# Sliding-window attention, then a squared-ReLU layer: two groups of x turned in another PSUM bank, and a new planned order

## The chip, the cores and the metric

The kernel runs on one core of a Trainium2 chip. The metric is device time in microseconds (us); of the kernel before, three timed runs gave a median of 291.02 us (290.34 to 291.29). About 0.9 us, 0.3%, is the least difference that a measurement of this kernel tells from none.

## What is computed

The reference, cut to what matters. There are 8 batches of 8 heads, 576 positions and 64 elements a head; the output of attention, laid out as 4608 tokens by 512, is the x of the second part.

```python
scores = (q @ k.T) / sqrt(64)                      # q, k, v: 8 x 8 x 576 x 64
scores = where(abs(i - j) <= 32, scores, -1e9)     # a band of 65 keys
attn   = softmax(scores) @ v
x      = attn.transpose(0, 2, 1, 3).reshape(4608, 512)
h      = x @ w_in                                  # 512 x 2048
g      = maximum(h, 0) ** 2
out    = g @ w_out                                 # 2048 x 512, float32 out
```

## The kernel before

**Attention** goes by groups G = 0 to 23 of 192 positions, three to a batch, all eight heads at once. The steps of a group have these names in the text below, and these lines in the profile:

- Loads of k, q and v issued by GpSimd (POOL; `load_qk` L477, `load_pair` L509, `load_v` L526). They cast float32 to bfloat16 on the way.
- Turning k and q: groups 0 to 5 on TensorE (turn k10 is that of k, batch 1, group 0, so G = 3; L568) into a PSUM bank, which ScalarE (ACT, L596 and L601) or VectorE (DVE, L599) then empties. From group 6 on the DMA queue of SyncE (SP) transposes them (L608).
- S, the scores: on PE, L649 for groups 0 to 2, in two halves SA and SB, and L697 after that. X is the exponential on ACT (L674, L711), M the multiplication with the mask on DVE (L679, L719, L725).
- PA and PB, the product with v on PE (L753). R and N on DVE (L772, L775) divide it by its sums and write xa and xb. Between PA and PB, Z clears half of a bank (ACT L783 or DVE L785). So PB can start only after N of PA and Z.
- T, the turning of x: group 0 in the banks ht0 and outp1; groups 1 and 2 on PE (Ta L833, Tb L838), into one bank, which ACT empties into the tile xt (XT, L850); from group 3 on by SP's transposes (L854, L857).

**The first product** (A, L879) takes x in tiles of 192, later 256 tokens, in eight blocks of eight matmuls a tile; each block fills a bank that ACT empties with a ReLU (L885). The square follows on DVE (L893) or ACT (L895). In the first three tiles three banks take turns (ht0, ht1, outp1). The first block of a tile needs the turned x of its last group: A384.0, the first of the third tile, needs XT of group 2.

**The second product** works on pairs of 128 tokens with seven products instead of eight (P1 to P7, L965; sums of g on DVE, L951), but for the first pair, which takes plain products (B, L905) into outp0 and outp1.

PSUM has eight banks here: four are attention's tile at (scores in all four, PA and PB in banks 2 and 3), two are ht0 and ht1, two are outp0 and outp1.

**The order** is not written out. Every step is recorded with a key (its due time in units of 64 tokens), a cost, and what it reads and writes; a planner then runs the five engines and the DMA queues in a small model, takes on each engine the ready step with the lowest key, and writes the instructions in that order, with waits on semaphores. Offsets per kind of step (OFFS), a penalty on the other engine for steps that may run on ACT or DVE (FLEX), noise on the keys (NOISE, SEEDS) and the modelled DMA rates and delays (QMOVE, TGAP, the SLACKs) all bend that order. An engine works through its instructions strictly in the written order, so a wait holds up all that stands behind it. While PE has little to do in the first 20 us, dummy matmuls (L405) fill it.

Of the kernel before, what the change touches and what calls it, by code (L numbers as in the profile page):

```python
# [19 lines left out]
RING = 1536  # L20
NV, NRAW = 6, 6
TG = 6
# [4 lines left out]
GFAR = 12  # L27
GATE = 'P{}B'
GD = 3
GK = 8.0  # L30
TDKEY = 6
XKEY = (0.2, 0.5)
QMOVE = 14.8
HMOVE = 27
# [12 lines left out]
LANDQ = 2000  # L47
PQ = 100
# [13 lines left out]
SWB = 180  # L62
HWQ = {'k': 'SP', 'q': 'SP'}
HWC = {"k": ("DVE", "ACT"), "q": ("ACT", "DVE")}
TILES = ((192, 2304), (256, 4608))
SEEDS = (54889, 73113, 37345, 76131, 20885, 97248, 47624, 10448, 1997, 7471, 50773, 3305, 47783, 64133, 39018, 28670, 69087, 23028, 92194, 70005)
NOISE = 0.0
NBIAS = 1
PKEY = 2
MKEY = (-9.5, -6.5)  # L70
# [3 lines left out]
IOTA = -1  # L74
OPENING = [('k', 1), ('w1', 0), ('v', 0, 0), ('q', 1), ('v', 0, 1), ('q', 2), ('w1', 1), ('q', 5),
# [7 lines left out]
PSTEP = 0.4  # L83
SLEAD = 2.5
MOE = -1
SQBEG = 768
# [6 lines left out]
TWKEY = 6  # L93
# [263 lines left out]
class Gen:  # L357
# [103 lines left out]

    def gate(self, G):
        if G < 6:
            return None
        return self.p.named[GATE.format(G - GD)] if G >= GFAR else self.moe
# [12 lines left out]

    def load_hw(self, t, g, key):

# [19 lines left out]
    def load_pair(self, t, b, g, key):  # L502

        t0, n = KC[g] if t == "k" else (192 * g, 192)
        h = n // 2
        G = 3 * b + g
        pr, raw = self.PR[t][G % NPR], self.RAW[t][G % NRAW]
        s = (self.q if t == "q" else self.k)[b][:, t0:t0 + n, :].rearrange("h (p r) d -> p h (r d)", r=2)
        self.p.rec("POOL", lambda e: e.dma_start(pr[0:h, :].rearrange("p (h c) -> p h c", c=128), s), writes=[("pr", t, G % NPR)],  # L509
                   dma=(f"{t}p{G % NPR}", G), key=key, dur=500 + 3 * h, move=(h // 2, PMOVE), name=f"{t}{b}{g}",  # L510
                   slack=LSLACK1 if b else 0)
        self.p.rec("DVE", lambda e: e.tensor_copy(raw[0:h, :, :].rearrange("p r (h d) -> p r h d", d=64),
                                                  pr[0:h, :].rearrange("p (h r d) -> p r h d", r=2, d=64)),
                   reads=[("pr", t, G % NPR)], writes=[("raw", t, G % NRAW, x) for x in range(2)], key=3 * G - LEAD - PKEY if b == 0 else key, dur=430,
                   name=f"c{t}{b}{g}")

    def load_v(self, b, g, key, js=(0, 1)):
        G = 3 * b + g
        vt = self.V[G % NV]
        for j in js:  # L520
            k0 = 192 * g - 32 + 128 * j
            lo, hi = max(k0, 0), min(k0 + 128, S_)
            if g and j == 0 and G < NVR:
                lo = k0 + 64
            n = hi - lo
            self.p.rec("POOL", lambda e, j=j, lo=lo, hi=hi, k0=k0: e.dma_start(  # L526
                vt[lo - k0:hi - k0, j, :, 0:64], self.v[b, :, lo:hi, :].rearrange("h p d -> p h d")),
                writes=[("v", G % NV, j)], dma=(f"v{G % NV}{j}", G), key=key, dur=500 + 3 * n, move=(n // 2, VMOVE),
                name=f"v{b}{g}{j}", after=self.gate(3 * b + g), slack=LSLACK if b > 1 else LSLACK1 * b)

    def copy_v(self, G, key):
# [86 lines left out]
    def scores(self, G, ws):  # L618
        b, g = divmod(G, 3)
        i = b % 2  # L620
        kt, qt = self.KT[i], self.QT[i]
        key = 3 * G - LEAD + 0.3 * ws[0]
        a = 192 * g
        reg = {w: w if len(ws) == 2 or G < NBIAS else 0 for w in ws}
        if G < NBIAS:
# [57 lines left out]
    def scores_steps(self, G):  # L683
        b, g = divmod(G, 3)
        i = b % 2
        kt, qt = self.KT[i], self.QT[i]
        key = 3 * G - LEAD
        a = 192 * g
        n = G % 2

# [38 lines left out]
    def pv(self, G, w):  # L729
        b, g = divmod(G, 3)  # L730
        n = 2 * G + w
        key = 3 * G - LEAD + 0.3 * w + 0.1
# [55 lines left out]

    def xturn(self, G):
        xa, xb = self.XA[G % 3], self.XB[G % 3]  # L790
        key = 3 * G - LEAD + 0.5
# [70 lines left out]
    def mm1(self, t0, n, ds, key):  # L862
# [26 lines left out]
        if SQBEG <= t0 < SQEND and k % SQMOD[1] in SQMOD[0]:  # L889
# [4 lines left out]
                   reads=[("rt", k % 4)], writes=wr, key=key, dur=dve(c), name=f"g{t0}.{d0}",  # L894
                   alt=("ACT", lambda e: e.activation(gt[:, d0:d0 + len(ds), r:r + n], rr, ACTF.Square), act(c), "g")  # L895
                   if "g" in FLEX else None)

    def mm2(self, u, seg, key):
        op, gt = self.OUTP[u % 2], self.GT
# [158 lines left out]
    def build(self):  # L1058
# [40 lines left out]
        for G in range(NG):  # L1099
            b, g = divmod(G, 3)  # L1100
            if b > 1:
                key = 3 * G - LEAD - (GK if G >= GFAR else AHEAD)
                for t in "kq":
                    at(key, self.load_pair if G < TG else self.load_qk, t, b, g, key)
                at(key, self.load_v, b, g, key)
                if g and G < NVR:
                    key = 3 * G - LEAD - 0.5 if G >= VCS else key
                    at(key + 0.01, self.copy_v, G, key - VKEY if G >= VCS else key)
            for t in "kq":
                key = 3 * G - LEAD - (0.6 if G < TG else TDKEY)  # L1110
                at(key, self.turn_pe if G < TG else self.turn_dma, t, b, g, key)
            for ws in ((0,), (1,)) if G < NSPLIT else ():
                at(3 * G - LEAD + 0.3 * ws[0], self.scores, G, ws)
            if G >= NSPLIT:
                at(3 * G - LEAD, self.scores_steps, G)
            for w in range(2):
                at(3 * G - LEAD + 0.3 * w + 0.1, self.pv, G, w)
            at(3 * G - LEAD + 0.5, self.xturn, G)
        t0 = 0
        while t0 < NTOK:  # L1120
            n = next(n for n, end in TILES if t0 < end)
            m = min(512 // n, 4)
            for d in range(0, 16, m):
# [57 lines left out]
```

## Time and profile before

| | |
|---|---|
| median of three timed runs | 291.02 us |
| the profiled execution | 292.3 us |
| its span, first to last instruction | 290.1 us |
| mean granted TensorE clock | 0.999 |
| busy share: PE, DVE, ACT, POOL | 98%, 72%, 71%, 37% |
| read from HBM, written | 36.70 MB, 9.44 MB |
| DMA rate over the span | 159 GB/s |

The profile is of one execution, which took 292.3 us; 2.2 us of them lie outside the span. PE's busy time is that of matmuls whose ends are modelled, and consecutive matmuls overlap, so a wait of PE shows in full only in the distance between starts. Times of single instructions are given from the span's start.

### The profile page before, as it was taken

What the parts mean: (1) busy time and instruction counts of PE and PEld (TensorE: products, weight loads), DVE (VectorE), ACT (ScalarE), POOL (GpSimd) and SP (SyncE); (2) the same over time, 40 slices, a digit from 0 to 9 for tenths busy, and PEclk for the clock granted to TensorE, in tenths of its full rate; (3) what the DMA queues carried; (4) which work ended last, traced back from release to release, by engine and by line L of the source; (5) the groups of instructions that cost most, each with busy time, mean ns of one, the idle gap of its engine ahead of it and who ended that gap; (6) DMA issues with size and microseconds to landing.
All of it is one profiled execution on the core that took longest, in us unless ns stands there. A gap on an engine that the chain in (4) does not pass through costs nothing.

```text
span 290.1 us, 8378 instructions
## 1 busy us (share of the span) xinstructions
PE 283.0 (98%) x3426; PEld 245.6 (85%) x3430; DVE 208.2 (72%) x451; ACT 206.3 (71%) x379; POOL 107.0 (37%) x143
## 2 busy tenths in 40 slices
PE   7988999999999999999999999999999999999996
PEld 2467885889999999999998898888888888988885
DVE  6668779878687878686968886766876877735263
ACT  3379987586989988778776677758687638688520
POOL 8986660141566066326415435606236000000000
PEclk9999999999999999999999999999999999999999
DMA  9999999999999999999999999999999921202024
GB/s 161 188 194 186 197 178 139 200 135 173 113 143 209 129 165 119 173 171 143 124 150 189 150 127 169 131 190 90 169 106 139 143 91 29 84 18 76 0 75 145
DMA packets 160645, 39.97 MB, mean 138 GB/s; under 512 B 149984, under 2 KB 156256, under 8 KB 160608
## 3 DMA queue, kind: packets, MB, share of 16 engines
q0 software_dynamic: 106016, 17.93, 94.2%
q1 hardware_dynamic: 49552, 12.47, 31.4%
q10 hardware_dynamic: 5040, 9.05, 9.8%
q8 instruction: 27, 0.44, 0.7%
q14 instruction: 10, 0.08, 0.1%
HBM read 36.70 MB, written 9.44 MB: 159 GB/s over the span
## 4 chain that ended last, share of the span: by engine, by line
PE 87%; DVE 6%; ACT 3%; DMA 1%; issue 1%; ACTq 0%; DVEq 0%
PE ht L879 39%; PE outp L965 29%; PE at L965 4%; PE at L753 4%; PE at L697 3%; PE outp L405 2%; DMA oe<-in_q_dram 1%; PE at L879 1%; PE outp L905 1%; PE outp L879 1%; DVE xa L775 1%; DVE tw L932 1%; ACT qt L596 1%; DVE kt L599 1%; ACT e L674 1%
## 5 line engine op out<-in xcount | busy, mean ns | idle before, releaser
L879 PE MATMUL ht<-xt,w 128*128 128x192 bf16 (+1 forms) x1248 | 135.9, 258 | 0.0
L879 PEld LDWEIGHTS ht<-xt,w 128*128 128x128 bf16 x1248 | 109.3, 98 | 7.9 <-ACT qt L596 0.3
L885 ACT ACTIVATE rt<-ht 128x384 bf16<-128x384 f32 (+1 forms) x156 | 82.4, 534 | 36.4 <-PE ht L879 31.4
L477 POOL DMA_DIRECT2D kraw<-in_k_dram x36 | 27.7, 775 | 113.1 <-PE at L753 54.6
L895 ACT ACTIVATE gt<-rt 128x384 bf16<-128x384 bf16 (+1 forms) x116 | 65.3, 569 | 4.4 <-ACT rt L885 1.5
L526 POOL DMA_DIRECT2D v<-in_v_dram x48 | 37.7, 793 | 0.0
L965 PE MATMUL outp<-w,gt 128*128 128x256 bf16 x240 | 31.1, 273 | 0.0
L965 PE MATMUL outp<-tw,gt 128*128 128x256 bf16 x240 | 31.1, 273 | 0.0
L965 PE MATMUL outp<-tw,ss 128*128 128x256 bf16 x240 | 30.5, 273 | 0.3 <-DVE ss L951 0.2
L893 DVE TENSOR_TENSOR gt<-rt 128x384 bf16<-128x384 bf16 (+1 forms) x52 | 19.9, 386 | 13.5 <-ACT rt L885 13.0
L477 POOL DMA_DIRECT2D qraw<-in_q_dram x36 | 27.7, 773 | 0.0
L711 ACT ACTIVATE e<-at 128x1024 bf16<-128x1024 f32 x21 | 21.4, 1020 | 7.3 <-PE at L697 7.0
L965 PEld LDWEIGHTS outp<-tw,ss 128*128 128x128 bf16 x240 | 22.9, 98 | 3.1 <-issue 0.3
L965 PEld LDWEIGHTS outp<-w,gt 128*128 128x128 bf16 x240 | 23.0, 98 | 3.0 <-ACT oe L915 0.5
L965 PEld LDWEIGHTS outp<-tw,gt 128*128 128x128 bf16 x240 | 22.9, 98 | 2.5
L985 DVE TENSOR_TENSOR oe<-outp,uu 128x256 f32<-128x256 f32 (+1 forms) x30 | 16.6, 554 | 8.2 <-ACT rt L885 4.9
L719 DVE TENSOR_TENSOR pt<-e,mask 128x1024 bf16<-128x1024 bf16 x21 | 14.5, 691 | 11.1 <-ACT e L711 11.0
L753 PE MATMUL at<-v,pt 128*128 128x66 bf16 x384 | 20.1, 194 | 0.1
L753 PEld LDWEIGHTS at<-v,pt 128*128 128x128 bf16 x384 | 17.8, 98 | 2.2 <-ACT at L783 0.4
L725 DVE TENSOR_TENSOR pt<-em,mask 64x512 bf16<-64x512 bf16 x42 | 17.6, 420 | 1.7 <-ACT em L714 0.3
L775 DVE TENSOR_TENSOR xa<-at,rs 64x512 bf16<-64x512 f32 x24 | 16.7, 695 | 1.1
L775 DVE TENSOR_TENSOR xb<-at,rs 128x512 bf16<-128x512 f32 x24 | 16.5, 686 | 0.8
(112 smaller groups left out, 321.8 us busy)
## 6 DMA issues: line engine op xcount, KB each, us to landing
out_dram<-oe ACTq DMA_DIRECT2D x34, 256.0 KB, 4.0
qraw<-in_q_dram POOLq DMA_DIRECT2D x36, 96.0 KB, 6.2
w<-in_moe_w_in_dram POOLq DMA_DIRECT2D x4, 512.0 KB, 11.1
v<-in_v_dram POOLq DMA_DIRECT2D x16, 128.0 KB, 7.8
w<-in_moe_w_out_dram POOLq DMA_DIRECT2D x4, 512.0 KB, 17.7
v<-in_v_dram POOLq DMA_DIRECT2D x16, 96.0 KB, 7.0
kraw<-in_k_dram POOLq DMA_DIRECT2D x12, 112.0 KB, 5.5
kraw<-in_k_dram POOLq DMA_DIRECT2D x12, 96.0 KB, 4.4
```

The lines of the kernel that those rows point to most:

```text
L477: self.p.rec("POOL", lambda e, j=j: e.dma_start(raw[0:h, j, :].rearrange("p (h d) -> p h d", h=8), s[:, j]), writes=[("raw", t, G % NRAW, ...
L526: self.p.rec("POOL", lambda e, j=j, lo=lo, hi=hi, k0=k0: e.dma_start(vt[lo - k0:hi - k0, j, :, 0:64], self.v[b, :, lo:hi, :].rearrange("h ...
L711: self.p.rec("ACT", lambda e: e.activation(e2[:], self.AT[:, 0:1024], ACTF.Exp, scale=0.125), reads=lo, writes=[("e", n)], key=key, dur=ac ...
L725: self.p.rec("DVE", lambda e, w=w, r=r, x=x, mm=mm: e.tensor_tensor(pt[x:x + 64, w, :, 0:64], e1[r:r + 64, :].rearrange("p (h q) -> p h q" ...
L753: mm = e.matmul(avp[:, c:c + VS], pt[:, 4 * (h % 2) + h // 2, :], vt[:, w, h, :], start=(w == 0 and y == 0), stop=True, skip_group_check=True)
L775: self.p.rec("DVE", lambda e: e.tensor_tensor(x[r0:128, :].rearrange("p (x y c) -> p x y c", x=2, y=4), av[:, :, :, 0:64], rb, ALU.mult), ...
L879: mm = e.matmul(ht[:, n * x:n * x + n], self.W1[:, ft, 128 * d:128 * d + 128], self.XT[:, ft, r:r + n], start=(ft == 0), stop=(ft == 3))
L885: self.p.rec("ACT", lambda e: e.activation(rt[:, 0:c], ht[:, 0:c], ACTF.Relu), reads=htag, writes=[("rt", k % 4)], key=key, dur=act(c), na ...
L893: self.p.rec("DVE", lambda e: e.tensor_tensor(gt[:, d0:d0 + len(ds), r:r + n], rr, rr, ALU.mult), reads=[("rt", k % 4)], writes=wr, key=ke ...
L895: alt=("ACT", lambda e: e.activation(gt[:, d0:d0 + len(ds), r:r + n], rr, ACTF.Square), act(c), "g")
L965: mm = e.matmul(op[:, 256 * half:256 * half + 256], a[:, d, :], w[:, d, :], start=first and d == 0, stop=d == 7, skip_group_check=True)
L985: self.p.rec("DVE", lambda e: e.tensor_tensor(out, src, other, ALU.add), reads=btags[bank] + rd, writes=wr, key=key + k * PSTEP - DLEAD, d ...
```

## The change

- The rows of x of groups 1 and 2 are turned in outp0, the first bank of the second product, and no longer in bank 2 of at. Steps that need outp0 (the turn of k of group 2, the first plain products) and steps that need bank 2 of at (PA and PB, scores from group 3 on) are ordered by the planner accordingly.
- The planner models the casting loads of batches 2 to 7 at 21.4 instead of 14.8 a unit of rows, and shorter delays behind loads and transposes. One load (k of group 4) stands earlier in the opening list.
- Offsets, penalties, noise and seeds are others, so the order is another on every engine. The instructions themselves are the same in kind and number, but for steps that may run on ACT or DVE and that changed sides: in the changed kernel ACT has three evictions of k where it had two, 23 of the second product's evictions of one product where it had 20, eleven Z where it had ten, and in all DVE has 48 squares where it had 52.
- New functions (`setup_w1s`, `mm1_tile`, `mm1_pair`: the first product by seven products) are recorded for no tile, since STR1 is empty; `pos` gives the same keys as before, since LGS is 0.

The diff, cut to its core:

```diff
-GK = 8.0
+GK = 7.5
 QMOVE = 14.8
+QM2 = 21.4
+TBK = 3
-TGAP = 28
+TGAP = 16
-TSLACK = 3500
-XSLACK = 2500
-LSLACK = 3000
+TSLACK = 2200
+XSLACK = 2000
+LSLACK = 1200
+STR1 = ()
-NOISE = 0.0
+NOISE = 0.2
-OFFS = {'S': 3.25, 'M': -1.5, 'g': 2.25, 'Z': -3.5, 'N': 2.75, 'cc.': -4.25, 'u': -2.75, 'X': 3.25, 'r': -2.25, 'c': -2.25}
+OFFS = {'S': 1.25, 'M': -4.25, 'g': 2.75, 'Z': -2.0, 'N': 0.25, 'cc.': -3.0, 'u': -2.0, 'X': 3.0, 'r': -2.75, 'c': -4.25}
-FLEX = {'g': 5.25, 'Z': 4.75, 'ev': 3.0, 'o': 6, 'p': 0.75}
+FLEX = {'g': 0.5, 'Z': 3.5, 'ev': 2.25, 'o': -2, 'p': 0.5}
...
     def load_qk(self, t, b, g, key):
...
-                       move=(h // 2, QMOVE), name=f"{t}{b}{g}{j}", after=self.gate(3 * b + g), slack=LSLACK if b > 1 else 0)
+                       move=(h // 2, QMOVE if b < 2 else QM2), name=f"{t}{b}{g}{j}", after=self.gate(3 * b + g), slack=LSLACK if b > 1 else 0)
...
     def xturn(self, G):
...
         if G < NXT:
-            ps = self.AT[:, 1024:1536].bitcast(BF16)
-            bank = self.half(2)
+            ps = (self.OUTP[0][:] if 0 < G < TBK else self.AT[:, 1024:1536]).bitcast(BF16)
+            bank = ["outp0"] if 0 < G < TBK else self.half(2)
```

Up to the end of PA of group 1 (the first row below) PE's order is the old one. From there PE's rows before were these; ht and outp1 are the banks of first-product blocks, kraw2 is k of group 2, xa1 and xb1 are x of group 1, and L649 is S of group 2.

```order
L753 MATMUL at<-v1,pt1 128x66 x8
L568 MATMUL outp0<-ident,kraw2 128x80 x8
L879 MATMUL outp1<-xt,w1 128x192 x8
L879 MATMUL ht0<-xt,w1 128x192 x8
L649 MATMUL at<-qt0,kt0 128x128 x8
L879 MATMUL ht1<-xt,w1 128x192 x8
L879 MATMUL outp1<-xt,w1 128x192 x8
L753 MATMUL at<-v1,pt1 128x66 x8
L649 MATMUL at<-qt0,kt0 128x128 x8
L879 MATMUL ht0<-xt,w1 128x192 x8
L833 MATMUL at<-ident,xa1 128x64 x4
L838 MATMUL at<-ident,xb1 128x128 x4
```

In the changed kernel (its lines are ten higher) the same stretch of PE reads:

```order
L763 MATMUL at<-v1,pt1 128x66 x8
L889 MATMUL outp1<-xt,w1 128x192 x8
L889 MATMUL ht0<-xt,w1 128x192 x8
L843 MATMUL outp0<-ident,xa1 128x64 x4
L889 MATMUL ht1<-xt,w1 128x192 x8
L889 MATMUL outp1<-xt,w1 128x192 x8
L763 MATMUL at<-v1,pt1 128x66 x8
L848 MATMUL outp0<-ident,xb1 128x128 x4
L889 MATMUL ht0<-xt,w1 128x192 x8
L578 MATMUL outp0<-ident,kraw2 128x80 x8
L889 MATMUL ht1<-xt,w1 128x192 x8
L889 MATMUL outp1<-xt,w1 128x192 x8
```

The two turns of x came forward: T1a stands two blocks behind PA, and T1b directly behind the PB whose result it turns. The turn of k of group 2 went from the first place to behind them, and both halves of S of group 2 to behind the rows shown.

The second place is PE around PB and T of group 2 (xa2, xb2), up to the first rows of the third tile, which are the blocks that follow L697, S of group 3. Before:

```order
L753 MATMUL at<-v2,pt0 128x66 x8
L879 MATMUL ht1<-xt,w1 128x192 x8
L879 MATMUL outp1<-xt,w1 128x192 x8
L833 MATMUL at<-ident,xa2 128x64 x4
L838 MATMUL at<-ident,xb2 128x128 x4
L879 MATMUL ht0<-xt,w1 128x192 x8
L697 MATMUL at<-qt1,kt1 128x64 x24
L879 MATMUL ht1<-xt,w1 128x192 x8
```

In the changed kernel (kraw3 and qraw3 are k and q of group 3):

```order
L843 MATMUL outp0<-ident,xa2 128x64 x4
L578 MATMUL at<-ident,kraw3 128x112 x8
L578 MATMUL at<-ident,qraw3 128x96 x8
L763 MATMUL at<-v2,pt0 128x66 x8
L889 MATMUL ht0<-xt,w1 128x192 x8
L848 MATMUL outp0<-ident,xb2 128x128 x4
L707 MATMUL at<-qt1,kt1 128x64 x24
L889 MATMUL ht1<-xt,w1 128x192 x8
```

Between PB and T2b stands one block now, where two stood, between T2b and A384.0 only S of group 3, and the turns of k and q of group 3 moved to right ahead of PB.

The third place is ACT behind the exponentials of group 2, up to XT of group 2 (xt<-at, now xt<-outp0). Before:

```order
L885 ACTIVATE rt2<-ht1 128x384
L885 ACTIVATE rt3<-outp1 128x384
L895 ACTIVATE gt<-rt3 128x2x192
L885 ACTIVATE rt0<-ht0 128x384
L895 ACTIVATE gt<-rt0 128x2x192
L885 ACTIVATE rt1<-ht1 128x384
L885 ACTIVATE rt2<-outp1 128x384
L850 ACTIVATE xt<-at 128x4x192
```

In the changed kernel:

```order
L793 ACTIVATE at<-zz 64x2x264
L895 ACTIVATE rt2<-outp1 128x384
L611 ACTIVATE kt1<-at 128x4x2x112
L606 ACTIVATE qt1<-at 128x4x2x96
L895 ACTIVATE rt3<-ht0 128x384
L905 ACTIVATE gt<-rt2 128x2x192
L860 ACTIVATE xt<-outp0 128x4x192
```

ACT now empties both turned tiles of group 3 right ahead of XT; before, k of group 3 was emptied by DVE and q some twelve rows earlier on ACT. In the same way the turned k of group 2 went from DVE to ACT. On POOL and SP the loads and transposes of one group, which stood k, k, q, q, v, v, are mixed.

More of the change, by code (lines that the diff above doesn't have):

```diff
@@ L33 @@
 QMOVE = 14.8
+QM2 = 21.4
+TBK = 3
+GDL = 0
 HMOVE = 27
@@ L82 @@
 LAGP = 8.0
-PSTEP = 0.4
-SLEAD = 2.5
+PSTEP = 0.45
+SLEAD = 3.5
 MOE = -1
-SQBEG = 768
+SQBEG = 1152
 ULATE = 28
@@ L460, in setup_k, with pos @@
         self.ms("DVE", [("ktpad", i, 1)], self.KT[i][:, :, 32 + S_:KW], 0.0, key)
+    def pos(self, G):
+        return 3 * G - LEAD - max(0, G - LG0) * LGS
     def gate(self, G):
@@ L513, in load_pair @@
                                                   pr[0:h, :].rearrange("p (h r d) -> p r h d", r=2, d=64)),
-                   reads=[("pr", t, G % NPR)], writes=[("raw", t, G % NRAW, x) for x in range(2)], key=3 * G - LEAD - PKEY if b == 0 else key, dur=430,
+                   reads=[("pr", t, G % NPR)], writes=[("raw", t, G % NRAW, x) for x in range(2)], key=self.pos(G) - PKEY if b == 0 else key, dur=430,
                    name=f"c{t}{b}{g}")
@@ new lines, in mm1_tile @@
+    def mm1_tile(self, t0, key):
+        r = t0 % RING
+        xt = self.XT
+        B = {(i, j): xt[:, 2 * i:2 * i + 2, r + 256 * j:r + 256 * j + 256] for i in range(2) for j in range(2)}
+        bt = {(i, j): [("xt", ((t0 + 256 * j) // 64 + x) % (RING // 64)) for x in range(4)] for i in range(2) for j in range(2)}
+        q5 = self.RAW["q"][5]
+        qt = self.QT[0][:].rearrange("p a c -> p (a c)")
+        T = [q5[:, 0, :], q5[:, 1, :], qt[:, 0:512], qt[:, 512:1024]]
+        T = [x.rearrange("p (f c) -> p f c", f=2) for x in T]
+        qtt = [(n, 0, g) for n in ("qt", "qh") for g in range(3)]
+        tt = [[("raw", "q", 5, 0)], [("raw", "q", 5, 1)], [("t1", 2)] + qtt, [("t1", 3)] + qtt]
+        for n, a, b, at, bt_ in ((0, B[0, 1], B[0, 0], bt[0, 1], bt[0, 0]), (1, B[1, 1], T[0], bt[1, 1], tt[0]),
+                                 (2, B[1, 1], B[0, 1], bt[1, 1], bt[0, 1]), (3, B[1, 0], T[1], bt[1, 0], tt[1])):
+            self.p.rec("DVE", lambda e, n=n, a=a, b=b: e.tensor_tensor(T[n], a, b, ALU.subtract), reads=at + bt_, writes=tt[n],
+                       key=key - 1.5 + 0.1 * n, dur=dve(512), name=f"t{n}.{t0}")
+        self.T1, self.t1tag, self.B1, self.b1tag = T, tt, B, bt
```

121 lines of the change are left out of this document (106 added, 15 removed), and 4 rows, old and new, of the table OPENING.

## The prediction, made before the changed kernel ran

> **What bounds the kernel now.** I read the page first, then the busy time by stages, the list of what PE waits for, and then the timelines of PE, DVE and ACT in the one stage where PE is not full. The page gives the bound at once:
>
> ```profile
> span 290.1 us, 8378 instructions
> PE 283.0 (98%) x3426; PEld 245.6 (85%) x3430; DVE 208.2 (72%) x451; ACT 206.3 (71%) x379; POOL 107.0 (37%) x143
> ```
>
> TensorE is busy for 98% of the span, and the change neither adds nor removes a matmul. So only waits of PE can come or go. The busy times by stages (length of the stage, then busy time of each engine) show where waits are:
>
> ```profile
> core 0: us, PE busy (x) PEld busy (x) DVE busy (x) ACT busy (x) POOL busy (x), PEclk, DMA share, GB/s
> 20.70:35.90 15.20, 14.19 (x227) 12.75 (x224) 12.78 (x27) 14.85 (x31) 9.87 (x14) 1.00 1.58 193
> 35.90:60.00 24.10, 23.80 (x297) 18.79 (x294) 19.31 (x41) 18.07 (x34) 7.91 (x11) 1.00 1.93 166
> 60.00:262.00 202.00, 201.70 (x2528) 182.04 (x2527) 150.04 (x312) 152.51 (x285) 70.88 (x93) 1.00 1.44 135
> ```
>
> From 60 to 262 us PE stands for 0.30 us in all, from 35.9 to 60 for 0.30, but from 20.7 to 35.9 for 1.01 us, and in that stage ACT is busy for 14.85 of 15.20 us. Before 20.7 us the order of PE is the old one. So the change is decided between 20.7 and 35.9 us, where x of groups 1 and 2 is turned. Whom PE waits for stands in its list of waits:
>
> ```profile
> PE at L833 <- DVE xb L775: 0.6, 1, 0.6
> ...
> PE at L697 <- ACT xt L850: 0.2, 1, 0.2
> ```
>
> The first is T1a before its x, the second S of group 3 behind the emptying of x of group 2, which lies in attention's bank. The other six entries end on DVE, ACT or issue, none on a transfer.
>
> **The change, part by part.** These are PE's rows (start, length with the pipeline's end, line) to which I compare: PA of group 1, the turn of k of group 2, two blocks A; then A0.12, T1a, T1b, A0.14, the turn of q of group 3; A192.14, S of group 3, A384.0; at last PB of group 3 and A576.0.
>
> ```profile
> 20.73 0.42 PE L753 MATMUL at<-v,pt 128*128 128x66 bf16 x8
> 20.98 0.45 PE L568 MATMUL outp<-ident,kraw 80*128 80x80 bf16 x8
> 21.27 0.83 PE L879 MATMUL outp<-xt,w 128*128 128x192 bf16 x8
> 21.93 0.82 PE L879 MATMUL ht<-xt,w 128*128 128x192 bf16 x8
> ...
> 25.14 0.83 PE L879 MATMUL ht<-xt,w 128*128 128x192 bf16 x8
> 26.58 0.29 PE L833 MATMUL at<-ident,xa 64*128 64x64 bf16 x4 [0.61 <-DVE xb L775]
> 26.80 0.40 PE L838 MATMUL at<-ident,xb 128*128 128x128 bf16 x4
> 27.03 0.82 PE L879 MATMUL ht<-xt,w 128*128 128x192 bf16 x8
> 27.97 0.50 PE L568 MATMUL at<-ident,qraw 96*128 96x96 bf16 x8
> ...
> 34.39 0.82 PE L879 MATMUL ht<-xt,w 128*128 128x192 bf16 x8
> 35.45 0.52 PE L697 MATMUL at<-qt,kt 64*128 64x64 bf16 x24 [0.24 <-ACT xt L850]
> 35.91 0.83 PE L879 MATMUL ht<-xt,w 128*128 128x192 bf16 x8
> ...
> 42.32 0.42 PE L753 MATMUL at<-v,pt 128*128 128x66 bf16 x8
> 53.79 1.40 PE L879 MATMUL ht<-xt,w 128*128 128x192 bf16 x15
> ```
>
> From start to start, PA or PB takes PE 0.25 us, a block A 0.66, T1a 0.22, T1b 0.23, the turn of 80 columns 0.29 (112 and 96 columns by that 0.41 and 0.35), S of group 3 0.46. What the old order loses here: T1a starts 0.78 us after A0.12 is through (25.14 + 0.66), the turn of q 0.28 after A0.14, S of group 3 0.40 after A192.14. That is 1.46 us. All three come from x turned in a bank of at: behind it stand the scores' and PA's use of that bank.
>
> The work of PE between PA of group 1 (20.73) and A384.0 is the same in both orders: 14 blocks, four PA or PB, three S, three turns of k or q, four T. So the start of A384.0 tells the loss. What the new order makes of it follows from DVE's and ACT's rows: R of group 1, a square, N of PB of group 1, R of PB of group 3; then XT of group 1, a ReLU, the emptying of a turned q.
>
> ```profile
> 21.62 0.21 DVE L772 RECIPROCAL rs<-at 64x8 f32<-64x8 f32 x1
> ...
> 24.50 0.36 DVE L893 TENSOR_TENSOR gt<-rt 128x384 bf16<-128x384 bf16 x1
> ...
> 25.84 0.69 DVE L775 TENSOR_TENSOR xb<-at,rs 128x512 bf16<-128x512 f32 x1
> ...
> 42.77 0.21 DVE L772 RECIPROCAL rs<-at 128x8 f32<-128x8 f32 x1
> ```
>
> ```profile
> 27.23 0.81 ACT L850 ACTIVATE xt<-at 128x768 bf16<-128x768 bf16 x1
> 27.94 0.48 ACT L885 ACTIVATE rt<-ht 128x384 bf16<-128x384 f32 x1
> 28.51 1.03 ACT L596 ACTIVATE qt<-at 128x768 bf16<-128x768 bf16 x1
> ```
>
> R starts 0.45 us after its PB (42.32 to 42.77) and takes 0.24 with the gap behind it, N 0.69, and T follows 0.05 after N (26.53 to 26.58). XT starts 0.43 after T1b and ends 0.81 later.
>
> - T1a: two blocks behind PA, PE is there at 20.73 + 0.25 + 2 x 0.66 = 22.30. DVE goes R (21.62), square, N, so xa1 is there at 21.62 + 0.24 + 0.36 + 0.69 + 0.05 = 22.96. Wait 0.66.
> - T1b: it stands directly behind the PB whose result it turns. From PB's start to T1b 0.45 + 0.24 + 0.69 + 0.05 = 1.43 must pass, PB is through after 0.25. Wait 1.18. Behind it, in order, stand A0.12 and all other work, which needed nothing of it.
> - Turn of k of group 2: it needs outp0, which now holds x until XT has read it: 0.43 + 0.81 + 0.05 = 1.29 after T1b; T1b and a block take 0.89. Wait 0.40. This is the change's own price: the bank saved in at is taken from k. S of group 2 follows without a wait, since two blocks cover the eviction of k (0.89 on ACT, below).
> - T2b: one block stands between PB and it. The path is 1.43 and one more square, 1.79; PB and the block take 0.91. Wait 0.88.
> - S of group 3 and A384.0: from the turn of k of group 3 on, ACT needs 0.54 to start (27.97 to 28.51), then evicts k and q, does a ReLU and a square, and XT of group 2, which A384.0 needs. The eviction of 896 columns on ACT is in no row; 640 took 0.89,
>
> ```profile
> L601 ACT ACTIVATE kt<-at 128x640 bf16<-128x640 bf16 x1 | 0.9, 886 | 0.6 <-PE at L568 0.6
> ```
>
> and 768 (of q) 1.03, so 0.14 a step of 128 makes 1.17; its bounds are 0.89 and 1.3. With 1.03, 0.48, a square taken like the ReLU, 0.81, less 0.10 of overlap at four places (27.23 + 0.81 against 27.94), ACT is through 0.54 + 3.57 = 4.11 after the turn. PE has 0.41 + 0.35 + 0.25 + 0.66 + 0.88 (the wait) + 0.23 + 0.46 = 3.24. Wait 0.9 for both. The Trainium skill ("ScalarE: Activation LUTs", rules for kernel authors) would price this eviction otherwise: about 0.3 us an ACTIVATE and 0.83 ns an element, an estimate of 1.04 us, and this wait would be 0.13 shorter; its figure for 768 columns, 0.94, is below the row's 1.03.
>
> Sum: 0.66 + 1.18 + 0.40 + 0.88 + 0.90 = 4.02, against 1.46 before: A384.0 comes 2.6 us later, at 38.5. The first three need only R, N and XT, as measured, so 2.2 is firm; the other two hang on a queue that I put together. Bounds: +0.8 with those two at nothing, +2.9 with the dearer eviction.
>
> After A384.0 the old order loses 0.60 us of visible PE idle time up to 262 us, and a new order can't win more than that. I credit half, 0.3, since I find no stall removed by name; bounds 0 and 0.6. The tail keeps its last six products. The loads' new rate I give nothing: no wait of PE ended on a transfer, so a better placed load has none to remove. What covers them is their lead. The one place where it nearly ends is A576.0, which needs x of group 3 by SP's transpose:
>
> ```profile
> 43.97 1.20 SPq L857 DMA_TRANSPOSE xt<-xb  x1
> DMA to landing us min/median/max: 8.3/8.3/8.3
> ```
>
> Issued 1.65 us after PB (42.32), it landed at 52.3, 1.5 ahead of A576.0. In the new order DVE evicts k of group 4 and copies a load between N of PA and R of PB, about 1.3 us; so it lands some 11.2 after PB, and A576.0 comes after 11.4. I take no wait there; 1 us more of DMA time would cost about 0.8, at most 1.1.
>
> In sum +2.6 - 0.3 = +2.3 us: span 290.1 + 2.3 = 292.4. The profiled execution took 292.3, which is 1.3 above the median of 291.02; that median plus 2.3 is **293.3 us**.
>
> **The rivals.**
> *The freed bank pays (faster).* PA of group 2 no longer waits for XT of group 1, nor S of group 3 for XT of group 2: the three old waits, 1.46 us, go. If no new wait came, the time would be 291.0 - 1.46 - 0.3 = 289.3. It decides at T1b: PE must come to it no sooner than 1.43 us after PB's start. For it: ACT is full in this stage, and PE could be late already. Against it: between PB and T1b stands nothing, and no row lets R and N be shorter. Chance 0.09.
> *The late half is hidden (same).* The waits at T2b and A384.0 vanish, because PE is behind already and ACT and DVE catch up meanwhile: 2.24 - 1.46 - 0.3 = +0.5, 291.5 us. For it: each early wait gives ACT as much time. Against: PB of group 2 and T2b again stand one block apart, and ACT took over two evictions of k. Chance 0.12.
> *Late x at A576.0 (slower still).* The transposes land 1 us later than reckoned: +2.3 + 1.1, 294.4 us. For it: that margin is some 0.2 us now. Against: fewer loads may be in flight by then. Chance 0.10.
> *The clock falls.* All stages above show PEclk 1.00, but no wait there is longer than 0.61 us, and the new ones reach 1.2, three or four within 12 us. At half speed from T1b to T2b the 10 blocks there would take 0.66 more each, 6.6 us: 299.9 us. Chance 0.02. The Trainium skill ("TensorE: Matmul & The Clock Gate", why this matters for your kernels) speaks against it: the clock is cut after gaps of more than some 3 us; no run here shows such a gap.
>
> **How the numbers follow.** My forecast has 0.67; it and the two slower rivals make slower by over 0.3% (291.9 us) 0.79, same 0.12, faster 0.09. The range goes down to the low bounds together, 0.8 - 0.6 = +0.2, 291.2, and up to the high ones, 2.9 + 1.1 = +4.0, 295.0. It leaves out the freed bank and the fallen clock, 0.11, and the far ends of the others.
>
> **What would show it.** Right: PE's timeline shows about 1.2 us from the end of PB of group 1 to T1b, with the idle time put down to DVE's xb; A384.0 starts near 38.5; A576.0 near 55; and between 60 and 262 us PE stands for under 0.6 us. Wrong at its root: A384.0 at or before 35.9, or T1b without a wait. Wrong in the rest: A384.0 near 38.5, but PE in the later stages faster by more than 0.6 us, which the old trace doesn't allow, or new waits there on transfers.

## The result, and the profile after

| | before | after |
|---|---|---|
| median of 20 runs each | 290.72 us (290.28 to 294.54) | 292.49 us (291.61 to 294.88) |
| ratio after to before, 95% interval | | 1.0067 (1.0046 to 1.0089) |
| the profiled execution, its span | 292.3, 290.1 us | 291.92, 289.8 us |
| PA of group 1 starts at | 20.73 us | 18.70 us |
| from there to A384.0 | 15.18 us | 17.97 us |
| from A384.0 to the last product | 250.39 us | 249.43 us |

The changed kernel is slower: the medians differ by 1.77 us, and the ratio is 1.0067. The two profiled executions hide that: that of before began PA of group 1 two microseconds later, with the same instructions ahead of it. Such late openings are a matter of the single run: of the fourteen executions profiled for this text three had PA of group 1 at 20.7 to 20.9 us, the others at 18.7 to 19.3, and that of before happened to be a late one. So the two are compared from PA of group 1 on: +2.79 up to A384.0, -0.96 behind it, +1.83 in all, which agrees with the measured 1.77.

The page of after, and the busy time by the same stages (stage, length, busy time of PE, PEld, DVE, ACT, POOL, the granted clock, and last the share and rate of the DMA engines):

```profile
span 289.8 us, 8372 instructions
PE 281.2 (97%) x3430; PEld 245.0 (85%) x3430; DVE 205.2 (71%) x442; ACT 211.2 (73%) x388; POOL 107.4 (37%) x143
```

```profile
18.68:36.67 17.99, 14.54 (x227) 12.68 (x225) 10.46 (x25) 17.06 (x34) 11.11 (x15) 1.00 1.59 191
36.67:60.00 23.33, 23.33 (x291) 18.54 (x292) 19.83 (x39) 19.13 (x37) 8.74 (x12) 1.00 1.88 163
60.00:262.00 202.00, 201.78 (x2532) 182.81 (x2530) 148.37 (x307) 155.05 (x291) 69.89 (x91) 1.00 1.45 135
```

In the stage up to A384.0 PE now stands for 3.45 us instead of 1.01; behind it, up to 262 us, for 0.22 instead of 0.60. ACT has 17.06 us of work in the first stage, 2.21 more than before, and DVE 10.46, 2.32 less. PE's rows in that stage, from T1a to A384.0:

```profile
20.98 0.29 PE L843 MATMUL outp<-ident,xa 64*128 64x64 bf16 x4 [0.54 <-DVE xa L785]
...
22.52 0.42 PE L763 MATMUL at<-v,pt 128*128 128x66 bf16 x8
23.97 0.40 PE L848 MATMUL outp<-ident,xb 128*128 128x128 bf16 x4 [1.03 <-DVE xb L785]
24.20 0.82 PE L889 MATMUL ht<-xt,w 128*128 128x192 bf16 x8
25.27 0.46 PE L578 MATMUL outp<-ident,kraw 80*128 80x80 bf16 x8 [0.24 <-ACT xt L860]
...
33.04 0.42 PE L763 MATMUL at<-v,pt 128*128 128x66 bf16 x8
33.30 0.82 PE L889 MATMUL ht<-xt,w 128*128 128x192 bf16 x8
34.58 0.40 PE L848 MATMUL outp<-ident,xb 128*128 128x128 bf16 x4 [0.47 <-DVE xb L785]
35.09 0.52 PE L707 MATMUL at<-qt,kt 64*128 64x64 bf16 x24
36.67 0.83 PE L889 MATMUL ht<-xt,w 128*128 128x192 bf16 x8 [1.06 <-ACT xt L860]
```

From start to start, less what the row ahead takes, PE loses 0.71 us at T1a, 1.20 at T1b (behind PB at 22.52), 0.41 at the turn of k of group 2, 0.62 at T2b, 0.28 at S of group 3, 1.12 at A384.0 and 0.28 at T2a and the two halves of S of group 2: 4.62 us. By the same count the old order loses 1.85: the 1.46 of the prediction, 0.21 at the first half of S of group 2, and 0.09 each at the second half and at T2a. The last wait, for XT of group 2, ends on ACT's row of work:

```profile
33.02 1.15 ACT L611 ACTIVATE kt<-at 128x896 bf16<-128x896 bf16 x1
34.03 1.00 ACT L606 ACTIVATE qt<-at 128x768 bf16<-128x768 bf16 x1
34.89 0.48 ACT L895 ACTIVATE rt<-ht 128x384 bf16<-128x384 f32 x1
35.39 0.52 ACT L905 ACTIVATE gt<-rt 128x384 bf16<-128x384 bf16 x1
35.82 0.79 ACT L860 ACTIVATE xt<-outp 128x768 bf16<-128x768 bf16 x1
```

T2b was through at 34.80, XT started at 35.82: ACT had the two evictions of group 3, a ReLU and a square ahead of it.

### The profile page after: what moved, and what is told of

It reads as the page before. It is cut to its first block, busy times and chain, and to the rows that moved or that the text cites. A ratio compares the mean times of both kernels' runs of the same rounds, so it can differ in the third digit from the quotient of the medians.

```text
span 289.8 us, 8372 instructions
## 1 busy us (share of the span) xinstructions
PE 281.2 (97%) x3430; PEld 245.0 (85%) x3430; DVE 205.2 (71%) x442; ACT 211.2 (73%) x388; POOL 107.4 (37%) x143
## 3 DMA queue, kind: packets, MB, share of 16 engines
q10 hardware_dynamic: 5040, 9.05, 10.4%
## 4 chain that ended last, share of the span: by engine, by line
PE 88%; ACT 6%; DVE 2%; DMA 1%; issue 1%; ACTq 1%; DVEq 0%
PE ht L889 38%; PE outp L1083 31%; PE at L1083 4%; PE at L763 4%; PE at L707 3%; PE outp L1023 2%; ACT rt L895 2%; DMA oe<-in_q_dram 1%; PE at L889 1%; ACT e L684 1%; ACT qt L606 1%; PE outp L889 1%; PE outp L412 1%; ACT kt L611 1%; ACTq L1131 1%
## 5 line engine op out<-in xcount | busy, mean ns | idle before, releaser
L905 ACT ACTIVATE gt<-rt 128x384 bf16<-128x384 bf16 (+1 forms) x120 | 68.0, 574 | 3.0
L487 POOL DMA_DIRECT2D kraw<-in_k_dram x36 | 28.5, 795 | 47.8 <-PE at L763 20.1
L536 POOL DMA_DIRECT2D v<-in_v_dram x48 | 38.3, 801 | 9.4 <-PE at L763 9.4
L903 DVE TENSOR_TENSOR gt<-rt 128x384 bf16<-128x384 bf16 (+1 forms) x48 | 18.1, 379 | 16.1 <-ACT rt L895 15.4
## 6 DMA issues: line engine op xcount, KB each, us to landing
w<-in_moe_w_out_dram POOLq DMA_DIRECT2D x4, 512.0 KB, 18.7
```

The lines of the kernel that those rows point to most:

```text
L903: self.p.rec("DVE", lambda e: e.tensor_tensor(gt[:, d0:d0 + len(ds), r:r + n], rr, rr, ALU.mult), reads=[("rt", k % 4)], writes=wr, key=ke ...
```

## The experiments

In the kernels below each engine takes its order from a list written into the kernel, no longer from the planner. The lists are those planned for the kernel before ("old") and the changed one ("new"), edited as shown; the work is the same in all. Names are those of the text above; the last rows of the opening are S of group 3 on PE, the ReLU of A192.14 or XT of group 2 on ACT, N of PB of group 2 on DVE.

**1. Opening and rest exchanged.**

```diff
 open_old
-all engines: new order; TBK = 3
+PE, ACT, DVE up to A384.0: old order; TBK = 1
+behind it, and POOL and SP: new order
```

> The changed kernel with the old opening: PE up to S of group 3, ACT up to the ReLU of A192.14 and DVE up to N of PB of group 2 stand in the order of the kernel before, and x of groups 1 and 2 is turned in bank 2 of at; all behind that, and POOL and SP as a whole, stand as in the changed kernel. Nothing is left out. From PA of group 1 to A384.0 the kernel before took 15.18 us and the changed one 17.97 (+2.79); from A384.0 to the last product it was 250.39 and 249.43 (-0.96). Theory (the loss sits in the opening, the gain in the rest, and neither needs the other): A384.0 15.2 us after PA, 0.96 under the kernel before, 289.8 us. Rival (the rest is only faster because a late opening gives ACT and DVE time to catch up): no gain, 290.7 us.

```diff
 open_new
-behind A384.0, and POOL and SP: new order
+behind A384.0, and POOL and SP: old order
```

> The reverse: the new opening (x of groups 1 and 2 in outp0) on PE, ACT and DVE, and the order of the kernel before behind it and on POOL and SP. Nothing is left out. Theory (opening and rest are separate): A384.0 18.0 us after PA of group 1, 2.8 over the kernel before, 293.5 us. Rival (the rest catches up by itself what a late opening loses): about the changed kernel's 292.5 us.

Measured: open_old 289.91 us against 290.76 for before on the same chip, ratio 0.9973 (0.9960 to 0.9986); A384.0 came 15.19 us after PA of group 1. open_new 293.31, ratio 1.0083 (1.0069 to 1.0098); A384.0 after 17.96. The two effects, -0.85 and +2.55, add up to 1.70, and the change as a whole made 1.77. So the loss sits in the opening, the gain behind it, and neither needs the other. In the single profile of open_old the gain behind A384.0 is less, 0.31 us (250.08 against 250.39), where the times have 0.85; half a microsecond of that gain is so not seen in this pair of profiles. Its list of waits shows two new waits:

```profile
PE at L578 <- DVE kraw L522: 0.7, 1, 0.7
PE ht L889 <- DMA w<-in_moe_w_in_dram: 0.7, 1, 0.7
```

The first is the turn of k of group 4. With the old opening PE comes to it 1.7 us sooner than in the changed kernel (39.88 against 41.55 us, the wait included), and the load of that k landed at 39.2 in both. The second is new to this text: A0.12 needs the last quarter of w_in. PE's rows around it in open_old (PB of group 1, S, A0.12, T1a):

```profile
22.50 0.42 PE L763 MATMUL at<-v,pt 128*128 128x66 bf16 x8
22.86 0.40 PE L659 MATMUL at<-qt,kt 64*128 64x128 bf16 x8
23.96 0.83 PE L889 MATMUL ht<-xt,w 128*128 128x192 bf16 x8 [0.71 <-DMA w<-in_moe_w_in_dram]
24.73 0.29 PE L843 MATMUL at<-ident,xa 64*128 64x64 bf16 x4
```

A0.12 waits 0.77 us here for a load that landed at 23.9, and T1a behind it only 0.11. In the profile of before, two microseconds late, the load was there ahead of A0.12 (23.95 against 25.14), and T1a waited 0.78. The two waits are nearly of one size, so that from PA to A384.0 it is 15.19 and 15.18 us; but in all four profiles with the old opening and an early start (open_old, bank_only and the two of run 7) the first wait is one for weights.

**2. The bank without the order.**

```diff
 bank_only
-all engines: new order
+all engines: old order, TBK = 3
...
-                key = self.pos(G) - (0.6 if G < TG else TDKEY)
+                key = -5.0 if (t, G) == ("k", 2) else self.pos(G) - (0.6 if G < TG else TDKEY)
```

> The order of the kernel before on every engine, and only x of groups 1 and 2 turned in outp0 instead of bank 2 of at (the turn of k of group 2 stays ahead of it). Nothing is left out. Theory (the order makes the loss, the bank by itself is worth the old wait at S of group 3): T1a comes before N of PB, S of group 3 no longer waits 0.40, A384.0 14.7 us after PA of group 1 instead of 15.2, time 290.2 us. Rival one (the bank makes the loss): at least the 0.41 that the turn of k of group 2 waited in the changed kernel, 291.1 us or more. Rival two (ACT is the second bound of this stage, 98% busy, and what PE gains it waits for ACT a few blocks later): A384.0 14.7 but the time within 0.2 of the kernel before, 290.5 to 290.9 us.

Measured: 290.57 us against 290.76, ratio 0.9993 (0.9973 to 1.0013). A384.0 came 14.97 us after PA of group 1, 0.21 sooner than before, and S of group 3 no longer waited; but A384.6 and A384.8 then waited 0.09 and 0.21 for ACT, and the first plain product came 21.04 us after PA, against 20.94. So the bank doesn't make the loss: rival one falls, and rival two, that ACT takes the gain back, is what the rows show.

**3. The order without the bank.**

```diff
 order_only (TBK = 1)
 PE: ... A0.6
-T1a
 A0.8 A0.10 PB(1)
+T1a
 T1b ... A192.12
-T2a
 turn k, q of 3, PB(2), A192.14
+T2a
 T2b S(3) A384.0
```

> The order of the changed kernel on every engine, with x of groups 1 and 2 in bank 2 of at as before. Since that bank is free for T1a and T2a only behind N of their PB, these two stand directly ahead of T1b and T2b. Nothing is left out. Theory (order): the waits of T1a (0.71) and of the turn of k of group 2 (0.41) go or shrink, the 1.19 ahead of the turned x of group 1 and the waits for XT of group 2 stay: A384.0 17.4 to 17.9 us after PA of group 1, 292.0 to 292.5 us. Rival (the bank makes the loss): A384.0 near 15.2, 289.8 us with the rest's gain.

Measured: 295.15 us, ratio 1.0149 (1.0110 to 1.0188), far over either theory. A384.0 came 17.88 us after PA, as the first theory has it. What is on top came behind it. PE at S of group 3, and the stages around it (the clock stands third from the end):

```profile
38.03 0.82 PE L707 MATMUL at<-qt,kt 64*128 64x64 bf16 x24 [1.65 <-ACT xt L860]
38.78 1.46 PE L889 MATMUL ht<-xt,w 128*128 128x192 bf16 x8
```

```profile
36.00:38.00 2.00, 0.38 (x6) 0.20 (x4) 0.39 (x2) 1.95 (x4) 0.00 (x0) 0.83 1.76 187
38.00:40.00 2.00, 1.97 (x32) 1.83 (x33) 0.45 (x2) 1.11 (x2) 0.00 (x0) 0.50 2.09 161
...
42.00:44.00 2.00, 2.00 (x16) 1.90 (x14) 0.71 (x2) 0.95 (x3) 0.79 (x2) 0.50 1.38 203
```

PE stood in one piece for 1.65 us by that row, 1.82 from start to start (S of group 3, in all four banks of at, must wait for XT of group 2), and the granted clock fell to 0.50 for 6.8 us; blocks that take 0.66 from start to start took 1.26. All six runs of this kernel had a mean clock of 0.988 to 0.994. Against the changed kernel this profile loses 3.5 us behind A384.0: 2.5 by 44 us, while the clock is low, and 1.1 at 90 to 92 us, where issuing two output transfers held ACT for 2.14 us. So the new order by itself loses what the changed kernel loses. In the changed kernel S, free to go, cuts the wait in two; that the new bank keeps the clock up in this way is what run 4 tries.

**4. Is it the wait in one piece?**

```diff
 one_wait
 PE: ... T2b
-S(3)
 A384.0
+S(3)
 A384.2 ...
```

> The changed kernel with A384.0 ahead of S of group 3 on PE, and the ReLU of A384.0 ahead of that group's exponentials on ACT; all else as changed. Nothing is left out. In the kernel with the new order and the old bank, PE stood 1.65 us in one piece ahead of S of group 3, and PEclk fell from 1.00 to 0.50 for some 6.5 us. In the changed kernel the same waiting is cut in two by S (0.47 ahead of T2b, 1.06 behind S). Here nothing cuts it: from T2b to A384.0 PE stands 1.7 us. Theory (a single wait of that length lowers the clock): PEclk 0.50 for about 6 us behind A384.0, 295 to 296 us. Rival (there the clock fell for the idle time of the whole stage, or by chance): PEclk 1.00, 292.5 to 293.4 us, the excess from the exponentials, which come 0.7 later.

The expectation names a move on ACT as well. The kernel that ran doesn't have it: its list for ACT is that of the changed kernel, and in its profile the ReLU of A384.0 (40.47 us) follows the two exponentials of group 3 (39.07 and 39.56), which here wait for S.

Measured: 295.72 us, ratio 1.0165 (1.0127 to 1.0202). PE stood 1.86 us from T2b to A384.0, and the clock fell:

```profile
36.00:38.00 2.00, 0.73 (x8) 0.63 (x8) 0.36 (x1) 1.22 (x2) 0.00 (x0) 0.95 1.78 181
38.00:40.00 2.00, 2.00 (x33) 1.66 (x32) 0.30 (x1) 0.93 (x2) 0.00 (x0) 0.50 2.12 166
40.00:42.00 2.00, 2.00 (x19) 1.93 (x18) 1.59 (x4) 2.00 (x5) 0.07 (x1) 0.70 2.01 174
```

So the clock falls here too, as the theory has it. But it is not all of the loss: one of the four runs took 295.53 us at a mean clock of 0.999, as long as the others. In the profile 2.1 of the 3.5 us lost behind A384.0, against the changed kernel, are lost by 41.4 us, and 1.4 at 90 and 185 us, each time behind the issue of an output transfer on ACT (1.22 and 2.48 us).

Nor does the length of the stand tell when the clock falls: in the profile of run 5 below one of 3.19 us left it at 1.00. The work ahead doesn't either. The fall came at 37.3 us in order_only, still inside the stand, and at 37.8 in one_wait; in the 3.4 us ahead of it PE was busy for 1.90 and 1.24 us. In the changed kernel it was busy for 1.77 in the 3.4 us up to A384.0, less than in order_only, and the clock stayed.

The Trainium skill ("TensorE: Matmul & The Clock Gate", Part 1 and its section on HAM oscillation) has the clock set by PE's activity in a free-running window of some 3.4 us, and asks kernels to avoid gaps longer than that. The runs differ from the rule on gaps, since a stand of 1.8 us was enough. The clock stood at 0.50 for 6.8 us in order_only and for 3.4 in one_wait, some two such windows and one, which agrees with what the Trainium skill says there of the window; where the windows lay in a run is not recorded.

A third kernel (order_split) was to take the long wait out of run 3:

```diff
 order_split (to order_only)
 PE: ... PB(2)
-A192.14
 T2a T2b
+A192.14
 S(3)
```

> The new order with x of groups 1 and 2 in the old bank (T1a and T2a directly ahead of T1b and T2b, as in the run in which the clock fell), but with A192.14 put between T2b and S of group 3 on PE, and its ReLU and the square behind it put behind XT of group 2 on ACT. Nothing is left out. No single wait should then be over some 1.5 us: about 1.2 to 1.45 at T2a, 0.4 at S of group 3. Theory (there the time over the changed kernel's was the clock alone, and a wait of up to 1.45 us doesn't lower it): PEclk 1.00, A384.0 16.9 to 17.4 us after PA of group 1, 291.6 to 292.5 us. Rival (the old bank with the new order is slow by itself, or 1.4 us is enough for the clock): 294 us or more.

Measured: 295.14 us, ratio 1.0135 (1.0087 to 1.0182). Here too the move on ACT that the expectation names is not in the kernel: XT of group 2 still stands behind the ReLU of A192.14 and the square, and these now had to wait for the later A192.14 (ReLU at 36.36 us, XT at 37.31). So S of group 3 waited 1.99 us, A384.0 came 19.41 us after PA, and the clock fell again, for 3.4 us (mean 0.988 to 0.994 in four of six runs). The run tests neither its theory nor its rival, and says nothing on the bank beyond run 3.

**5. Old loads and transposes under the new order.**

```diff
 loads_old
-POOL, SP: new order
+POOL, SP: old order
```

> The changed kernel with POOL's and SP's instructions (loads and transposes) in the order of the kernel before. PE, ACT and DVE as changed, nothing is left out. Theory (the loads' new rate and the order that it plans are worth nothing): 292.3 to 292.7 us. Rival (the gain of 0.96 behind A384.0 comes from better placed loads and transposes): 293.3 us or more.

Measured: 295.51 us, ratio 1.0154 (1.0118 to 1.0190): 3.0 us slower than the changed kernel, against the theory. Up to A384.0 nothing differs (17.97 us after PA). Nearly all of the time goes in one place, A3072.0, which waits for the x of group 17. In loads_old PE (PA of group 18, then A3072.0 and the next block), and SP's issue of that transpose:

```profile
190.70 0.42 PE L763 MATMUL at<-v,pt 128*128 128x66 bf16 x8
194.15 1.91 PE L889 MATMUL ht<-xt,w 128*128 128x256 bf16 x16 [3.03 <-DMA xt<-xa]
```

```profile
178.62 4.92 SPq L618 DMA_TRANSPOSE kt<-kraw  x2
183.63 3.84 SPq L618 DMA_TRANSPOSE qt<-qraw  x2
187.56 1.20 SPq L864 DMA_TRANSPOSE xt<-xa  x1
```

In the changed kernel the same rows are:

```profile
190.28 0.42 PE L763 MATMUL at<-v,pt 128*128 128x66 bf16 x8
190.54 1.91 PE L889 MATMUL ht<-xt,w 128*128 128x256 bf16 x16
```

```profile
182.40 1.18 SPq L618 DMA_TRANSPOSE kt<-kraw  x1
183.67 1.20 SPq L864 DMA_TRANSPOSE xt<-xa  x1
```

The new order brings A3072.0 five products forward on PE, and SP has x of group 17 ahead of two of the four transposes of k and q of group 19. With the old SP order it stands behind all four and is issued 3.9 us later. The rival's time, 293.3 us or more, came in, but its reason is too small: the gain behind A384.0 was 0.96 and the loss here 3.0. What the run shows is that the new order of PE needs the new order of SP's transposes at this place; that the loads on POOL matter is not shown, since both were exchanged at once.

**6. Single waits of the new opening.**

```diff
 t1b_later
 PE: ... PB(1)
-T1b
 A0.12
-turn of k of group 2
 A0.14
+T1b
+turn of k of group 2
```

> The changed kernel with T1b and the turn of k of group 2 moved on PE behind A0.12 and A0.14, so that two blocks stand between PB of group 1 and T1b; all else as changed. Nothing is left out. Theory one (the wait of 1.19 at T1b is a loss by itself, as the sum of the prediction has it): T1b waits under 0.1, A384.0 1.1 us earlier, 291.4 us. Theory two (what stands behind needs XT of group 1 anyhow: the turn of k through outp0, A192.0 through its x, S of group 2 through k; the wait only moves there): 0 at T1b, 1.0 to 1.1 at the turn of k, A384.0 within 0.2 of the changed kernel's, 292.3 to 292.7 us.

Measured: 293.98 us, ratio 1.0117 (1.0080 to 1.0154), and A384.0 19.25 us after PA, 1.3 later than in the changed kernel. PE from PB of group 1 on (then two blocks, T1b, the turn of k):

```profile
22.85 0.42 PE L763 MATMUL at<-v,pt 128*128 128x66 bf16 x8
24.27 1.48 PE L889 MATMUL ht<-xt,w 128*128 128x192 bf16 x16 [1.00 <-DMA w<-in_moe_w_in_dram]
25.59 0.39 PE L848 MATMUL outp<-ident,xb 128*128 128x128 bf16 x4
26.88 0.46 PE L578 MATMUL outp<-ident,kraw 80*128 80x80 bf16 x8 [0.90 <-ACT xt L860]
```

Theory one falls. Theory two is right that the wait moves to the turn of k (1.06), but both missed that A0.12 can't go ahead of the load of w_in: it waits 1.16 in T1b's stead, and T1b comes 1.3 late. In the changed kernel T1b waits to 23.97 us, and that load landed at 24.00. So in a run with an early opening A0.12 could hardly have gone sooner, and T1b's wait costs next to nothing by itself.

```diff
 xt_first
 ACT: ... eviction of q of group 3
+XT(2)
 ReLU of A192.14, square
-XT(2)
```

> The changed kernel with XT of group 2 moved on ACT ahead of the ReLU of A192.14 and the square behind it; all else as changed. Nothing is left out. XT then starts as soon as T2b is through, about 0.8 us earlier. Theory one (PE's wait at A384.0 is the loss, and its start tells the loss): A384.0 0.8 us earlier, 291.7 us. Theory two (ACT is the second bound of this stage: the work put behind XT still stands ahead of the ReLU that empties A384.0's bank): A384.0 0.8 us earlier, but A384.6 waits 0.6 to 0.7 for that ReLU, and the time is within 0.2 of the changed kernel's 292.5.

Measured: 292.79 us, ratio 1.0079 (1.0041 to 1.0116). A384.0 came 17.15 us after PA, 0.82 sooner, but A384.6 after 19.86, against 19.96:

```profile
36.00 0.83 PE L889 MATMUL ht<-xt,w 128*128 128x192 bf16 x8 [0.27 <-ACT xt L860]
...
38.70 0.83 PE L889 MATMUL ht<-xt,w 128*128 128x192 bf16 x8 [0.56 <-ACT rt L895]
```

Theory two: the ReLU that empties A384.0's bank stands behind the same ACT work, and the time is not told from that of the changed kernel.

```diff
 evk10_dve
-ACT: ... Z(2) ReLU, eviction of k of group 3, eviction of q
+ACT: ... Z(2) ReLU, eviction of q
 DVE: ... N of PB(2)
+eviction of k of group 3
```

> The changed kernel with the emptying of the turned k of group 3 on DVE, behind N of PB of group 2, as the kernel before had that work on DVE; ACT has 1.15 us less ahead of XT of group 2. All else as changed, nothing is left out. Theory two of the run before (ACT is the second bound): XT comes 1.1 us earlier, S of group 3 now waits for k on DVE instead, A384.0 0.5 to 0.7 earlier with no wait behind it, 291.8 to 292.2 us. Rival (the loss sits in PE's waits for turned x of groups 1 and 2, and ACT's share is hidden): within 0.2 of 292.5.

Measured: A384.0 17.50 us after PA, 0.47 sooner; from there to A384.6 no wait was over 0.06, and A384.6 came 0.41 sooner too. S of group 3 now waits for the k on DVE, 0.92 from start to start:

```profile
37.91 0.53 PE L707 MATMUL at<-qt,kt 64*128 64x64 bf16 x24 [0.75 <-DVE kt L609]
```

That is the theory's place, and just under its size of 0.5 to 0.7. The time doesn't tell: 292.87 us, ratio 1.0065 (1.0028 to 1.0102), and the changed kernel's 1.0067 lies in that interval; in the profiled execution the issue of an output transfer held ACT for 1.5 us at 85 us, and PE lost 0.82 us behind it.

**7. What beats both.**

```diff
 bank_rest (to open_old)
-TBK = 1
+TBK = 3, turn of k of group 2 recorded ahead as in bank_only
 bank_rest_k
 POOL: ... 
+k of group 4
 second quarter of w_out
-k of group 4
```

> The old opening with only the bank changed (x of groups 1 and 2 in outp0, the turn of k of group 2 ahead of it as before), and everything behind A384.0, with POOL and SP as a whole, as in the changed kernel. Nothing is left out. Theory (the old opening stands against two loads, whatever the bank: the last quarter of w_in landed at 24.0 us, ahead of A0.12, and k of group 4 at 39.2, ahead of its turn, which waited 0.90 us with the old opening): within 0.2 of the 289.9 us that the old opening with the old bank took. Rival (the bank is worth its 0.4 at S of group 3): 289.5 us.

> The same, with one load moved: k of group 4 is issued ahead of the second quarter of w_out instead of behind it. Nothing is left out. Theory (the wait for that load is a real loss): k lands 1.4 us earlier, the wait of 0.9 at its turn goes, at most 0.3 comes back at the turn of q or at A576.0, 289.2 to 289.5 us. Rival (another load or ACT takes its place at once): within 0.2 of the same kernel without the move.

Measured: bank_rest 290.00 us against 290.70, ratio 0.9974 (0.9955 to 0.9994); bank_rest_k 290.07, ratio 0.9982 (0.9958 to 1.0005). That nothing more is to be had, the theory of the first and the rival of the second, came in: A384.0 was again 0.2 sooner with the new bank and A384.6 was not (17.40 against 17.31 us after PA); with the load moved, the wait at the turn of k of group 4 fell from 0.59 to 0.08 and 0.29 came up at the turn of q. The old opening with the new order behind it is faster than both kernels, though against the kernel before by no more than 0.26 to 0.27%, 0.7 to 0.85 us, with intervals (of open_old and bank_rest) that end at 0.9986 and 0.9994. The bank doesn't matter to it.

## Why the prediction was right, and where not

- **The whole.** Forecast 293.3 us in a range of 291.2 to 295.0, measured 292.49, on the side that had 0.79. Of the 0.8 between them 0.3 is the base (20 runs have before at 290.72, the three first ones at 291.02); the rest is the gain behind A384.0, 0.66 more than forecast, less the 0.2 that the opening lost more.
- **T1a, T1b, turn of k of group 2:** 0.66, 1.18 and 0.40 forecast, 0.71, 1.20 and 0.41 measured. The path from PB by R and N to T1b took 1.45 us, 1.43 forecast.
- **T2b** was over-sized: 0.88 forecast, 0.62 measured. The square between R and N hardly lengthened that path:

```profile
33.49 0.21 DVE L782 RECIPROCAL rs<-at 128x8 f32<-128x8 f32 x1 [0.38 <-PE at L763]
33.62 0.31 DVE L903 TENSOR_TENSOR gt<-rt 128x384 bf16<-128x384 bf16 x1
33.84 0.68 DVE L785 TENSOR_TENSOR xb<-at,rs 128x512 bf16<-128x512 f32 x1
```

N started 0.35 us after R, where the forecast had 0.60; alone it follows after 0.24.
- **S of group 3 and A384.0** were under-sized: 0.90 forecast, 1.40 measured. ACT sets the end, so what T2b didn't wait was waited here, and ACT began 0.2 later, behind a ReLU. The eviction of 896 columns took 1.15 us; the forecast had 1.17 by the rows' step. By the figures of the Trainium skill ("ScalarE: Activation LUTs", rules for kernel authors), which it gives there for a bias that is a pointer operand, the estimate was 1.04, so the rows were nearer.
- **The sum up to A384.0:** +2.6 forecast, +2.79 measured. The waits that it names came to 4.34 us, 0.3 over its 4.02; it left out small waits at T2a and S of group 2, 0.39 in the old order and 0.28 in the new. The upper bound of +2.9 doesn't follow from its reason: an eviction of 1.3 us instead of 1.17 makes 2.7. The sum was right by a route that is only half the truth. The prediction added PE's waits as if each were a loss. Runs 2 and 6 show that taking such a wait away moves it, to ACT or to a load: ACT is a second bound of this stage, busy for 17.06 of 17.99 us. It has 2.21 us more work there; the evictions of k of groups 2 and 3, 0.88 and 1.15 us, which DVE did before, are 2.03 of it. That this work is the cause is shown for one eviction only, and for 0.47 of its 1.15 us (evk10_dve); the rest is argued from the size.
- **"All three come from x turned in a bank of at"**, said of the old waits, does not hold for the second, the turn of q. In the profile that was read, that turn, at 27.97 us, starts just behind DVE's copy of the loaded q,

```profile
27.41 0.42 DVE L512 COPY qraw<-tw 96x1024 bf16<-96x1024 bf16 x1
```

and in bank_rest, with x in outp0, it still waits 0.30. For the first it holds in the late run that was read; in an early one A0.12's wait for w_in stands there, and "none ends on a transfer" is then wrong. That the size was the same is luck.
- **The rest:** -0.3 forecast with 0.6 as its bound, -0.96 in the profiles, -0.85 in run 1: the step that failed. The bound was read from PE's idle time as the stages show it, 0.60 us; but consecutive matmuls overlap, and from start to start the old order loses 1.93 us behind A384.0, in nine places of 0.09 to 0.38, at the second product's first pairs above all. One of them, with 0.22 shown of 0.38:

```profile
64.64 0.41 PE L753 MATMUL at<-v,pt 128*128 128x66 bf16 x8
65.28 1.05 PE L965 MATMUL outp<-tw,ss 128*128 128x256 bf16 x8 [0.22 <-DVE ss L951]
```

The new order has one such place left, 0.38 at 149.6 us. The difference of the two lists, 1.55, is more than the 0.96 that came; the remaining 0.6 was not traced.
- **The loads' new rate, credited with nothing:** no run shows a wait of the old order that it removes. That the new order of PE leans on the new order of SP's transposes (run 5) was not seen.
- **A576.0:** no wait, as forecast; x landed 10.4 us after PB, not 11.2, so the margin was 1.0, not 0.2.
- **The rivals.** *The freed bank pays* falls at T1b, the place named; run 2 puts the bank at nothing. *The late half is hidden* falls: 2.02 us were waited at T2b, S of group 3 and A384.0, which were to go. *Late x at A576.0* falls. *The clock falls*, at 0.02, was held too cheap: two of the 20 runs of the changed kernel had a mean clock of 0.994 (294.2 and 294.9 us), and three other orders of the same stage brought it down in 13 of 16 runs. Four more runs of the changed kernel took 294.2 to 294.8 us at a clock of 1.00; none of them was profiled.

## What to carry to other kernels

Before a wait of the bound engine is counted as a loss, ask who would be late next if it went: here a second engine at 95% in the same stage, and a load that lands at a fixed time, took back what moving single waits gained. Read idle time from start to start, not from the busy share, when ends overlap; and compare two executions from the first point where their orders differ, since a single profile can carry a late opening. An order of one queue belongs to the order of the engine that it feeds, and is not exchanged by itself.

## What the runs showed of the hardware

- One stand of PE of 1.8 to 2.0 us, from start to start, went with a fall of the granted clock to 0.50 for 3.4 or 6.8 us (order_only, one_wait, order_split; the mean clock was down in 13 of 16 runs). A stand of 3.19 us at 191 us in the profile of loads_old left it at 1.00; three other runs of the five had a mean clock of 0.994, and where it fell in them is not known. What decides between the cases stays open.
- The issue of an output transfer on ACT took 0.36 us in the median, but 1.0 to 2.5 us in 15 cases out of 490, at 84 to 102, 146 to 154 and 180 to 192 us, and in ten of the fourteen profiles; in xt_first two of them in a row (2.33 us together) held up ACT, and PE behind it by 1.3 us at A1152.0 and the product after it. The cause was not tried.

```profile
83.25 2.33 ACTq L1131 DMA_DIRECT2D out_dram<-oe  x2
85.64 0.49 ACT L895 ACTIVATE rt<-ht 128x384 bf16<-128x384 f32 x1 [2.44 <-PE at L707]
```
